# 600 slots per expert instead of 608, outputs turned in 64-row halves, and a plain product for the last tile of a threshold attention with hash-routed experts

## The chip, the core and the metric

The kernel runs on one core of a Trainium2 chip. The core has TensorE (PE: matrix products and transposes, with its weight loads shown as PEld), VectorE (DVE), ScalarE (ACT), GpSimd (POOL) and SyncE (SP); POOL and SP issue most of the DMAs. PE writes only PSUM; DVE and ACT bring results from PSUM to SBUF.

The metric is device time in microseconds. Three timed runs of the kernel before gave 958.95, 956.51 and 956.54: median 956.54 us. One more execution was recorded by the profiler, which lengthens it a little.

## What is computed

First attention with a threshold, for 8 batches, 8 heads, 576 positions and 64 dimensions: scores that lie more than `tau` under the largest of their row are left out. Its output, turned to 4608 rows of 512, goes through a mixture of 8 experts, in which the token's id alone picks the expert.

```python
scores = scale * np.matmul(q, k.transpose(0, 1, 3, 2))
thresh = np.max(scores, axis=-1, keepdims=True) - tau
scores = np.where(scores >= thresh, scores, -1000000000.0)
...
expert_idx = token_ids * np.int64(2654435761) % np.int64(E)
for e in range(E):
    mask = expert_idx == e
    xe = x[mask]
    h = np.maximum(xe @ w1[e], 0.0)      # w1[e]: 512 x 1024
    out[mask] = h @ w2[e]                # w2[e]: 1024 x 512
```

The inputs are made with a fixed seed. The experts get between 533 and 599 of the 4608 tokens.

## The kernel before

**Attention** takes about the first half. It goes over 32 pairs of heads in steps that are written out by hand; PE computes scores (L219), turns the weights in halves of 64 rows (`turn`, L260 to L267) and multiplies by `v` (L297), while DVE and ACT work on rows of 576. Between these steps the generator `route()` (L350) runs small DVE operations that give every token a slot: expert times `CAP` plus its rank in the expert. Tokens beyond `CAP` of an expert go to overflow tiles. `scatters()` (L483) writes each token's number into a table of slots in DRAM, and the table is read back in an order of blocks of 32 slots; copies on DVE make the index tiles `gidx` and `gidx_x` of it (L744 to L750).

**The experts** follow one another. An expert has `CAP` = 608 slots in 19 blocks of 32: five tiles of rows, of 128, 128, 128, 128 and 96. `gather` fetches the rows of `x` by an indirect DMA of POOL, DVE turns them in squares of 32 and SP moves the squares into `xT` (L908 to L923).

Each of the two layers of an expert is a two-by-two block product with seven block products in place of eight (`seven`, L825). The slots are cut in two halves of `CH` = 304 columns. `left` and `right` prepare the sums of blocks on DVE; `left` writes one of them, s1, over the block a21 of the weights. A block product fills a PSUM tile `bank2` (two banks; four such tiles) and DVE adds it up. After each of six steps `seven` calls a function that puts other work in between. Layer 1 makes `h_0` (1024 x 608), layer 2 makes `oT` (512 x 608). An expert has 2 x 56 matrix products of 304 columns, except expert 0, whose first layer is a plain product that begins beside attention (`early_h`, `late_h`).

**The output.** `put_out` (L876) turns a tile of `oT` with four transposes of 128x128 (L882), copies the result to `o_sb` (ACT at L890; for the last expert also DVE at L888), and `put_rows` (L893) scatters the rows to `out` by an indirect DMA of POOL. The tiles of expert e are put out during the first layer of expert e + 1: two after step 0, two after step 1, one after step 2. For the last expert, tiles 0 and 1 follow step 4 of its second layer and the others the end of it (L970, L977). All this stands under a manual schedule: instructions go to the engines in the order in which the code makes them.

**The overflow loop** (L989) comes last; it runs once for each overflow tile. With no overflow tile it is skipped, but POOL and the other engines still wait in its exit for all DMAs.

Of the kernel before, what the change touches and what calls it, by code (L numbers as in the profile page):

```python
# [9 lines left out]
FP32 = mybir.dt.float32  # L10
# [10 lines left out]
def kernel(  # L21
# [12 lines left out]
    nc = tc.nc  # L34
# [28 lines left out]
    NSLOT = -(-(E * CAP + NOV * P) // P) * P  # L63
    BIG = 1 << 20
# [63 lines left out]
    with tc.tile_pool(name="a_q", bufs=1) as a_q, \  # L128
# [221 lines left out]
        def route():  # L350
# [39 lines left out]
            for e in (0, E // 2):  # L390
# [6 lines left out]
                if e == 0:  # L397
# [54 lines left out]
            nc.vector.tensor_scalar(out=ovt[:], in0=ovt[:], scalar1=float(P),  # L452
                                    scalar2=float((E - 1) * CAP), op0=ALU.mult, op1=ALU.add)
            yield
# [28 lines left out]
        def scatters():  # L483

            for c in range(NTC):
                nc.gpsimd.indirect_dma_start(
                    out=slot_dram[c % 2][:, :],
                    out_offset=bass.IndirectOffsetOnAxis(ap=slot_i[:, c:c + 1], axis=0),
                    in_=tok[:, c:c + 1], in_offset=None, bounds_check=NSLOT - 1,
                    oob_is_err=False)  # L490
                yield
            for _ in range(4):
                yield
            for table, dst in zip(slot_dram, sidx):
                slots = table[0:CAP].rearrange("(c s) o -> c (s o)", c=32)
                for h in range(4):
                    nc.sync.dma_start(out=dst[32 * h:32 * h + 32, 0:(NB - h + 3) // 4],
                                      in_=slots[:, h::4])
            for table, dst in zip(slot_dram, (stok, stok_odd)):
                for h in range(HP):  # L500
                    nc.sync.dma_start(
                        out=dst[32 * h:32 * h + 32],
                        in_=table[0:E * CAP].rearrange("(e c s) o -> c e (s o)", e=E, c=32))
# [121 lines left out]
        with tc.manual_schedule():  # L625
# [133 lines left out]
    with tc.tile_pool(name="m_x", bufs=1) as m_x, \  # L759
# [5 lines left out]
        xq = m_x.tile([P, DIN // 32, 32 * KT], FP32, name="xq")  # L765
        oT = m_x.tile([P, CO, CAP], FP32, name="oT")
        mark = m_x.tile([P, 1], FP32, name="mark")
# [4 lines left out]
        p1, u2, u3, u4 = (m_s.tile([P, 2, CH], FP32, name=n) for n in ("p1", "u2", "u3", "u4"))  # L772

# [3 lines left out]
        def sub(out, in0, in1):  # L777
            return lambda: nc.vector.tensor_tensor(out=out, in0=in0, in1=in1, op=ALU.subtract)
# [3 lines left out]

        def left(a11, a12, a21, a22, s):

            s2, s3, s4 = s
            return [sub(s3, a11, a21), add(a21, a21, a22), sub(s2, a21, a11), sub(s4, a12, s2)]

# [13 lines left out]

        def h_blocks(c0, c1):
            return [h_0[:, FH * j + c0:FH * j + c1, CH * k:CH * k + CH]
                    for j in range(2) for k in range(2)]

        def triple(t, c0, c1):
            return [t[:, i, c0:c1] for i in range(3)]

# [3 lines left out]
        def sums_w2(e):  # L812
            return left(*w2_blocks(w_tiles[e, 2]), triple(w2_s, 0, FH))

        def sums_x(e):
            return right(*x_blocks(xT_bufs[e % 2]), triple(x_s, 0, C2))

        def sums_h(c0, c1):
            return right(*h_blocks(c0, c1), triple(h_s, c0, c1))

# [4 lines left out]
        def seven(a, a_s, b, b_s, m0, outs, relu, after):  # L825

            (a11, a12, s1, a22), (s2, s3, s4) = a, a_s
            (b11, t1, b21, b22), (t2, t3, t4) = b, b_s
            c11, c12, c21, c22 = outs
            n_k = a11.shape[1]  # L830

            def product(x, y):
                ps = bank2()
                for i in range(2):
                    c0 = m0 + P * i
                    for c in range(n_k):
                        nc.tensor.matmul(ps[:, i, 0:CH], lhsT=x[:, c, c0:c0 + P], rhs=y[:, c],  # L837
                                         start=c == 0, stop=c == n_k - 1)
                return ps[:, :, 0:CH]
# [7 lines left out]
            nc.scalar.copy(p1[:], product(a11, b11))  # L847
            out(c11, product(a12, b21), p1[:], 0)
            add(u2[:], product(s2, t2), p1[:])()
            after(1)  # L850
            add(u3[:], product(s3, t3), u2[:])()
            after(2)
            out(c21, product(a22, t4), u3[:], 3)
            k5 = product(s1, t1)
            add(u4[:], k5, u2[:])()
            out(c22, k5, u3[:], 4)
            out(c12, product(s4, b22), u4[:], 5)

# [9 lines left out]
        def layer2(e, side):  # L868

            w = w_tiles.pop((e, 2))  # L870
            outs = [oT[:, C2 * i:C2 * i + C2, CH * k:CH * k + CH]
                    for i in range(2) for k in range(2)]
            seven(w2_blocks(w), triple(w2_s, 0, FH), h_blocks(0, FH), triple(h_s, 0, FH), 0, outs,
                  False, side)

        def put_out(e, kts):  # L876

            tr = bank2()
            for i, kt in enumerate(kts):
                rows = TROWS[kt]  # L880
                for co in range(CO):
                    nc.tensor.transpose(tr[0:rows, i, P * co:P * co + P],  # L882
                                        oT[:, co, FIRST[kt]:FIRST[kt] + rows], ident[:])
            for i, kt in enumerate(kts):
                rows = TROWS[kt]
                o_sb = m_o.tile([P, DIN], FP32, name="o_sb")
                if e == E - 1 and kt % 2:
                    nc.vector.tensor_copy(o_sb[0:rows], tr[0:rows, i])  # L888
                else:
                    nc.scalar.copy(o_sb[0:rows], tr[0:rows, i])  # L890
                put_rows(o_sb[0:rows], gidx[0:rows, e, kt:kt + 1])
# [33 lines left out]
        with tc.tile_pool(name="ps_x", bufs=1, space=PSUM) as ps_x, tc.manual_schedule():  # L925
            run(sums_w2(0), 4)
            fill(18)
            late_h(lambda fo: (ps_sc.tile([P, 2, 512], FP32, name="sc") if fo in (2, 4) else
                               ps_x.tile([P, 2, 512], FP32, name="xT_ps")))
            fetch(1)  # L930
            run(sums_h(0, FH), 4)
        sc_stack.close()
        ps_m = [ctx.enter_context(tc.tile_pool(name="ps_m", bufs=4, space=PSUM))]

        with tc.manual_schedule():
            for e in range(E):
# [3 lines left out]
                if e > 0:  # L940
                    w2_work, h_work = sums_w2(e), sums_h(0, 2)

# [14 lines left out]
                    layer1(e, side1)  # L957
                    run(sums_h(2, FH), 4)
                if e + 2 < E:
# [3 lines left out]
                def side2(step):  # L963
# [25 lines left out]
        with tc.For_i(0, n_ov, 1) as it:  # L989
# [12 lines left out]
            for table, dst in zip(slot_dram, (idx, idx_odd)):  # L1002
                nc.gpsimd.dma_start(out=dst[:], in_=table[bass.ds(it * P + E * CAP, P), :])
            nc.vector.tensor_tensor(out=idx[:], in0=idx[:], in1=idx_odd[:], op=ALU.min)
# [48 lines left out]
```

## Time and profile before

| | |
|---|---|
| median of three runs | 956.54 us |
| the profiled execution | 963.93 us, its span 962.3 us |
| granted clock of TensorE | 0.997 |
| busy over the span: PE, PEld, DVE, ACT, POOL | 98%, 67%, 77%, 50%, 31% |
| attention, from the start to about | 475 us |
| end of expert 0's first layer, start of the block products | 503.9 us |
| the last block product ends about | 950.0 us |
| block products in all (L837) | 1680 records of PE |
| output transposes (L882) | 160 records, 273 ns each as shown |

An instruction of PE with 32-bit operands appears as two records when it is a product and as one when it is a transpose. Records of PE overlap in the pipeline, so that the length shown for one (419 ns for a product of 304 columns) is more than the distance to the next; the distance is what counts. In the profile's shapes, `64*128` is a product that uses 64 of the array's 128 rows, `128*64` one that uses 64 of its columns, and `128*128` one that uses all.

### The profile page before, as it was taken

The page shows a single profiled execution, that of the slowest core. Times are in us where ns is not written, and L with a number is a line of the kernel's source. Part 1 is how long each engine was busy: PE and PEld are TensorE (multiplying, and loading weights), DVE is VectorE, ACT ScalarE, POOL GpSimd, SP SyncE. Part 2 cuts the span into 40 slices and gives each one's busy share as a digit, 9 for nine tenths or more (in the row PEclk, how much of TensorE's full clock was granted, in tenths as well). Part 3 has the DMA queues.
Part 4 walks back from the last instruction along what each step waited for, and adds up shares of the span by engine and source line. Part 5 has one row for each costly group of instructions (what it writes and reads, how often), then busy time and mean ns, then how long its engine had stood idle before and what let it go on. Part 6 is the DMA issues. An engine that isn't in the chain of part 4 may idle for free.

```text
span 962.3 us, 20672 instructions
## 1 busy us (share of the span) xinstructions
PE 941.3 (98%) x7595; PEld 646.8 (67%) x7595; DVE 738.2 (77%) x1631; ACT 479.6 (50%) x777; POOL 302.4 (31%) x413
## 2 busy tenths in 40 slices
PE   7999999999999999999999999999999999999995
PEld 4666666666566666656667777777777777777774
DVE  8999999999999999999446666756657556675541
ACT  6988898888888888888220211202112031120310
POOL 4233233346666633564043300303013030100202
PEclk9999999999999999999999999999999999999998
DMA  7445445544546857631016444344433445211101
GB/s 181 97 121 146 116 111 141 135 111 110 125 99 177 212 154 199 157 93 32 26 45 208 161 106 159 95 141 161 129 127 103 140 152 158 108 53 25 50 1 50
DMA packets 113397, 113.41 MB, mean 118 GB/s; under 512 B 27476, under 2 KB 87896, under 8 KB 113296
## 3 DMA queue, kind: packets, MB, share of 16 engines
q1 hardware_dynamic: 105168, 92.95, 35.7%
q0 software_dynamic: 7696, 18.91, 6.4%
q8 instruction: 62, 1.02, 0.4%
q14 instruction: 39, 0.32, 0.1%
q10 hardware_dynamic: 432, 0.21, 0.1%
HBM read 81.99 MB, written 21.85 MB: 108 GB/s over the span
## 4 chain that ended last, share of the span: by engine, by line
PE 79%; issue 16%; DVE 1%; ACT 1%; POOL 1%; DMA 1%; SPq 0%; POOLq 0%; DVEq 0%; ACTq 0%
PE bank L837 29%; PE av L297 18%; PE sc L219 15%; PE tr L266 11%; PE sc L578 3%; PE av L266 2%; PE bank L882 1%; POOL out_dram L894 1%; ACT w L244 1%; DVE w L255 1%; PE xT_ps L595 0%; PE sc L595 0%; DVE ns L230 0%; ACT wT_b L287 0%; DMA out_dram<-o_sb,gidx 0%
## 5 line engine op out<-in xcount | busy, mean ns | idle before, releaser
L244 ACT ACTIVATE w<-ns,nmx 128x576 f32<-128x576 f32 x288 | 220.4, 777 | 27.0 <-DVE ns L230 26.8
L255 DVE SCALAR_TENSOR_TENSOR w<-ns,thr,w 128x576 f32<-128x576 f32 x288 | 225.4, 815 | 0.0
L230 DVE TENSOR_SCALAR_CACHE_REDUCE ns<-sc 128x576 f32<-128x576 f32 x288 | 205.6, 746 | 7.5 <-PE sc L219 6.7
L219 PE MATMUL sc<-k_sb,q 64*128 64x288 f32 (+1 forms) x1280 | 177.2, 421 | 1.2 <-DVE drop L641 0.5
L266 PEld LDWEIGHTS tr<-ident,w 64*128 64x128 f32 x2624 | 106.1, 139 | 95.5 <-ACT wT_b L287 32.2
L237 POOL TENSOR_SCALAR thr<-nmx,drop 128x2 f32<-128x2 f32 (+1 forms) x160 | 103.8, 649 | 189.3 <-DVE ns L230 176.7
L266 PE MATMUL tr<-ident,w 64*128 64x64 f32 x2624 | 139.6, 231 | 6.6 <-ACT wT_b L287 2.6
L894 POOL DMA_INDIRECT out_dram<-o_sb,gidx x40 | 47.9, 1198 | 302.0 <-ACT o_sb L890 294.7
L847 ACT COPY p<-bank 128x608 f32<-128x608 f32 x22 | 14.6, 665 | 205.1 <-PE bank L837 205.0
L219 PEld LDWEIGHTS sc<-k_sb,q 64*128 64x128 f32 (+1 forms) x1280 | 92.9, 177 | 21.8 <-DVE ns L230 8.1
L837 PE MATMUL bank<-h,w_sb 128*128 128x304 f32 x384 | 101.0, 419 | 0.9 <-DVE h L600 0.9
L297 PE MATMUL av<-wT_a,v 128*64 128x320 f32 (+1 forms) x704 | 100.4, 418 | 0.0
L844 ACT ACTIVATE h<-h 128x608 f32<-128x608 f32 x56 | 39.8, 710 | 114.6 <-DVE h L781 111.9
L287 ACT COPY wT_a<-tr 128x512 f32<-128x512 f32 (+1 forms) x128 | 81.7, 639 | 20.5 <-PE tr L266 20.2
L837 PEld LDWEIGHTS bank<-h,w_sb 128*128 128x128 f32 x384 | 72.9, 190 | 26.5 <-DVE h L600 1.4
L837 PE MATMUL bank<-xT,w_sb 128*128 128x304 f32 x336 | 90.5, 419 | 0.0
L287 ACT COPY wT_b<-tr 128x512 f32<-128x512 f32 (+1 forms) x128 | 81.3, 635 | 16.0 <-PE tr L266 8.9
L297 PE MATMUL av<-wT_b,v 128*64 128x256 f32 x640 | 83.2, 389 | 0.0
L837 PEld LDWEIGHTS bank<-xT,w_sb 128*128 128x128 f32 x336 | 63.8, 190 | 22.1
L837 PE MATMUL bank<-h_s,w_s 128*128 128x304 f32 x256 | 66.8, 419 | 0.0
L297 PEld LDWEIGHTS av<-wT_a,v 128*64 128x64 f32 x704 | 43.8, 136 | 28.5
L781 DVE TENSOR_TENSOR u<-bank,u 128x608 f32<-128x608 f32 x44 | 34.3, 780 | 35.1 <-PE bank L837 35.0
(139 smaller groups left out, 1141.0 us busy)
## 6 DMA issues: line engine op xcount, KB each, us to landing
w_sb<-in_moe_w_dram SPq DMA_DIRECT2D x16, 2048.0 KB
q<-in_q_dram SPq DMA_DIRECT2D x62, 288.0 KB
v<-in_v_dram SPq DMA_DIRECT2D x32, 256.0 KB
x_scratch<-xm SPq DMA_DIRECT2D x32, 256.0 KB
xT<-xq SPq DMA_DIRECT2D x84, 80.0 KB
k_sb<-in_k_dram SPq DMA_DIRECT2D x31, 144.0 KB
k_sb<-in_k_dram SPq DMA_DIRECT2D x32, 112.0 KB
x_scratch<-xg SPq DMA_DIRECT2D x9, 256.0 KB
```

The costliest lines, as they stand in the source:

```text
L219: nc.tensor.matmul(sc[out_rows, i, 0:S2], lhsT=q_sb[rows, h, q0:q1], rhs=k_sb[rows, h], start=True, stop=True)
L230: nc.vector.tensor_scalar(out=ns[:].rearrange("p (i s) -> p i s", i=2), in0=sc[:, :, 0:S2], scalar1=-1.0, scalar2=None, op0=ALU.mult, op1= ...
L237: nc.gpsimd.tensor_scalar(out=thr[:, 0:j + 1], in0=stats[n][0][:, 0:j + 1], scalar1=drop[:], scalar2=None, op0=ALU.add)
L244: nc.scalar.activation(w, nss[n, j][:], AF.Exp, bias=stats[n][0][:, j:j + 1], scale=-1.0)
L255: nc.vector.scalar_tensor_tensor(out=w, in0=nss.pop((n, j))[:], scalar=stats[n][1][:, j:j + 1], in1=w, op0=ALU.is_le, op1=ALU.mult, accum_ ...
L266: nc.tensor.transpose(dst[:, r, 64 * c:64 * c + 64], src[rows, c0:c0 + P], ident[rows, rows])
L287: nc.scalar.copy(dst, tr[:, :, 0:64 * n_c].rearrange("p r (c q) -> p r c q", c=n_c))
L297: nc.tensor.matmul(av[64 * j:64 * j + 64, g, c0:c1], lhsT=v_sb[:, c, 64 * j:64 * j + 64], rhs=wT[g][:, i, c0:c1], start=(c == 0), stop=stop)
L781: return lambda: nc.vector.tensor_tensor(out=out, in0=in0, in1=in1, op=ALU.add)
L837: nc.tensor.matmul(ps[:, i, 0:CH], lhsT=x[:, c, c0:c0 + P], rhs=y[:, c], start=c == 0, stop=c == n_k - 1)
L844: nc.scalar.activation(c, c, AF.Relu)
L894: inst = nc.gpsimd.indirect_dma_start(out=out[:, :], out_offset=bass.IndirectOffsetOnAxis(ap=idx, axis=0), in_=o_sb, in_offset=None, bound ...
```

## The change

- `CAP` becomes 600. The table keeps 19 blocks of 32 slots (`SL` = 608) for an expert, but the last block holds only 24: a slot's place skips one in 18 beyond rank 456. Three more DVE operations in `route()` compute that. The halves `CH` become 300 columns and the last tile has 88 rows.
- `put_out` turns each 128x128 piece as two pieces of 64 rows, which go to the two banks of the PSUM tile; the copies to `o_sb` put them together in runs of 64.
- For the last expert, layer 2 runs on 480 slots only (halves `CHL` = 240). The remaining 120 slots are a plain product with the slots as the stationary operand (`last_tile`), so that their output needs no transpose: 8 products of 384 columns, then 8 of 128. In the middle of the first eight, `put_out` turns tiles 1, 2 and 3. So that the plain product finds the weights unchanged, s1 of that expert goes to a spare buffer of `w1_sb`.
- `gidx` of the last expert's tile 4 gets the indexes of the last four blocks: four more small copies.

```diff
-    CAP = 32 * NB
+    SL = 32 * NB
+    CUT = 8
+    CAP = SL - CUT
+    FULL = NB * (32 - CUT)
...
+            nc.vector.tensor_scalar(out=rank_f[:], in0=rank[:], scalar1=float(-1 - FULL), scalar2=0.0,
+                                    op0=ALU.add, op1=ALU.max)
...
-            nc.vector.tensor_scalar(out=first[:], in0=eidf[:], scalar1=float(CAP), scalar2=None,
+            nc.vector.tensor_scalar(out=rank_i[:, 0], in0=rank_f[:], scalar1=57.0, scalar2=None,
                                     op0=ALU.mult)
+            nc.vector.tensor_scalar(out=rank_i[:, 0], in0=rank_i[:, 0], scalar1=10, scalar2=None,
+                                    op0=ALU.logical_shift_right)
...
+            nc.vector.scalar_tensor_tensor(out=first[:], in0=eidf[:], scalar=float(SL),
+                                           in1=rank_i[:, 0], op0=ALU.mult, op1=ALU.add)
...
+                nc.vector.tensor_copy(gidx[rows, E - 1, KT - 1:KT],
+                                      stok[rows, E - 1, NB - 4 + h:NB - 3 + h])
...
+        CHL = 32 * (NB - 4) // 2
...
+            s1 = None
+            if e == E - 1:
+                spare = w_pool.tile([P, CO, F], FP32, name="w1_sb")
+                s1 = w_tiles["s1"] = spare[:, :, 0:D2]
+            return left(*w2_blocks(w_tiles[e, 2]), triple(w2_s, 0, FH), s1)
...
+        def last_tile(middle):
+
+            w, o_sb, idx = w_tiles[E - 1, 2], o_end, gidx[:, E - 1, KT - 1:KT]
+            rows = CAP - 2 * CHL
+            for c0, c1 in ((0, DIN - P), (DIN - P, DIN)):
+                ps = bank2()
+                for fo in range(FO):
+                    nc.tensor.matmul(ps[0:rows, 0, 0:c1 - c0], lhsT=h_0[:, fo, 2 * CHL:CAP],
+                                     rhs=w[:, fo, c0:c1], start=fo == 0, stop=fo == FO - 1)
+                    if (c0, fo) == (0, FH - 1):
+                        middle()
+                nc.scalar.copy(o_sb[0:rows, c0:c1], ps[0:rows, 0, 0:c1 - c0])
+            put_rows(o_sb[0:rows], idx[0:rows])
...
-                    nc.tensor.transpose(tr[0:rows, i, P * co:P * co + P],
-                                        oT[:, co, FIRST[kt]:FIRST[kt] + rows], ident[:])
+                    for r in range(2):
+                        half, c0 = slice(64 * r, 64 * r + 64), D2 * i + 64 * co
+                        nc.tensor.transpose(tr[0:rows, r, c0:c0 + 64],
+                                            oT[half, co, FIRST[kt]:FIRST[kt] + rows],
+                                            ident[half, half])
...
+                dst = o_sb[0:rows].rearrange("p (c r q) -> p r c q", c=CO, r=2)
+                src = tr[0:rows, :, D2 * i:D2 * i + D2].rearrange("p r (c q) -> p r c q", c=CO)
...
-                        put_out(e, (0, 1))
+                        put_out(e, (0,))
...
-            put_out(E - 1, (2, 3))
-            put_out(E - 1, (4,))
+            def middle():
+                put_out(E - 1, (1, 2))
+                put_out(E - 1, (3,))
+
+            last_tile(middle)
```

More of the change, by code (lines that the diff above doesn't have):

```diff
@@ L62 @@
     NOV = 32
-    NSLOT = -(-(E * CAP + NOV * P) // P) * P
+    NSLOT = -(-(E * SL + NOV * P) // P) * P
     BIG = 1 << 20
@@ L446, in route @@
             nc.vector.tensor_copy(rank[:], rank_i[:, 1])
+            nc.vector.tensor_scalar(out=rank_f[:], in0=rank[:], scalar1=float(-1 - FULL), scalar2=0.0,
+                                    op0=ALU.add, op1=ALU.max)
             yield
             nc.vector.tensor_copy(ovt[:], rank_i[:, 2])
-            nc.vector.tensor_scalar(out=first[:], in0=eidf[:], scalar1=float(CAP), scalar2=None,
+            nc.vector.tensor_scalar(out=rank_i[:, 0], in0=rank_f[:], scalar1=57.0, scalar2=None,
                                     op0=ALU.mult)
+            nc.vector.tensor_scalar(out=rank_i[:, 0], in0=rank_i[:, 0], scalar1=10, scalar2=None,
+                                    op0=ALU.logical_shift_right)
             yield
             nc.vector.tensor_scalar(out=ovt[:], in0=ovt[:], scalar1=float(P),
-                                    scalar2=float((E - 1) * CAP), op0=ALU.mult, op1=ALU.add)
+                                    scalar2=float(E * SL - CAP), op0=ALU.mult, op1=ALU.add)
+            nc.vector.scalar_tensor_tensor(out=first[:], in0=eidf[:], scalar=float(SL),
+                                           in1=rank_i[:, 0], op0=ALU.mult, op1=ALU.add)
             yield
@@ L494, in scatters @@
             for table, dst in zip(slot_dram, sidx):
-                slots = table[0:CAP].rearrange("(c s) o -> c (s o)", c=32)
+                slots = table[0:SL].rearrange("(c s) o -> c (s o)", c=32)
                 for h in range(4):
@@ L502, in scatters @@
                         out=dst[32 * h:32 * h + 32],
-                        in_=table[0:E * CAP].rearrange("(e c s) o -> c e (s o)", e=E, c=32))
+                        in_=table[0:E * SL].rearrange("(e c s) o -> c e (s o)", e=E, c=32))
             for _ in range(4):
@@ L766 @@
         oT = m_x.tile([P, CO, CAP], FP32, name="oT")
+        o_end = m_x.tile([P, DIN], FP32, name="o_end")
         mark = m_x.tile([P, 1], FP32, name="mark")
@@ L771 @@
         h_s = m_s.tile([P, 3, FH, CH], FP32, name="h_s")
-        p1, u2, u3, u4 = (m_s.tile([P, 2, CH], FP32, name=n) for n in ("p1", "u2", "u3", "u4"))
+        halves = [m_s.tile([P, 2, CH], FP32, name=n) for n in ("p1", "u2", "u3", "u4")]
+        CHL = 32 * (NB - 4) // 2
         def bank2():
@@ L781, in add, with left @@
             return lambda: nc.vector.tensor_tensor(out=out, in0=in0, in1=in1, op=ALU.add)
-        def left(a11, a12, a21, a22, s):
+        def left(a11, a12, a21, a22, s, s1=None):
+            s1 = a21 if s1 is None else s1
             s2, s3, s4 = s
-            return [sub(s3, a11, a21), add(a21, a21, a22), sub(s2, a21, a11), sub(s4, a12, s2)]
+            return [sub(s3, a11, a21), add(s1, a21, a22), sub(s2, s1, a11), sub(s4, a12, s2)]
         def right(b11, b12, b21, b22, t):
@@ L800, in x_blocks, with h_blocks, triple, half2 @@
             return [x[:, C2 * j:C2 * j + C2, CH * k:CH * k + CH] for j in range(2) for k in range(2)]
-        def h_blocks(c0, c1):
-            return [h_0[:, FH * j + c0:FH * j + c1, CH * k:CH * k + CH]
+        def h_blocks(c0, c1, half):
+            return [h_0[:, FH * j + c0:FH * j + c1, half * k:half * k + half]
                     for j in range(2) for k in range(2)]
-        def triple(t, c0, c1):
-            return [t[:, i, c0:c1] for i in range(3)]
+        def triple(t, c0, c1, width=None):
+            return [t[:, i, c0:c1, 0:width] for i in range(3)]
+        def half2(e):
+            return CH if e < E - 1 else CHL
         def sums_w1(e):
@@ L812, in sums_w2, with sums_h @@
         def sums_w2(e):
[L813 removed]
+            s1 = None
[3 more added lines that the diff above has]
+            return left(*w2_blocks(w_tiles[e, 2]), triple(w2_s, 0, FH), s1)
         def sums_x(e):
             return right(*x_blocks(xT_bufs[e % 2]), triple(x_s, 0, C2))
[L818 to L819 removed]
+        def sums_h(e, c0, c1):
+            return right(*h_blocks(c0, c1, half2(e)), triple(h_s, c0, c1, half2(e)))
         def run(work, n=1):
@@ L829, in seven @@
             c11, c12, c21, c22 = outs
-            n_k = a11.shape[1]
+            n_k, width = a11.shape[1], b11.shape[2]
+            p1, u2, u3, u4 = (t[:, :, 0:width] for t in halves)
             def product(x, y):
@@ L836, in product @@
                     for c in range(n_k):
-                        nc.tensor.matmul(ps[:, i, 0:CH], lhsT=x[:, c, c0:c0 + P], rhs=y[:, c],
+                        nc.tensor.matmul(ps[:, i, 0:width], lhsT=x[:, c, c0:c0 + P], rhs=y[:, c],
                                          start=c == 0, stop=c == n_k - 1)
-                return ps[:, :, 0:CH]
+                return ps[:, :, 0:width]
             def out(c, ps, u, step):
@@ L845, in out @@
                 after(step)
-            nc.scalar.copy(p1[:], product(a11, b11))
-            out(c11, product(a12, b21), p1[:], 0)
-            add(u2[:], product(s2, t2), p1[:])()
+            nc.scalar.copy(p1, product(a11, b11))
+            out(c11, product(a12, b21), p1, 0)
+            add(u2, product(s2, t2), p1)()
             after(1)
-            add(u3[:], product(s3, t3), u2[:])()
+            add(u3, product(s3, t3), u2)()
             after(2)
-            out(c21, product(a22, t4), u3[:], 3)
+            out(c21, product(a22, t4), u3, 3)
             k5 = product(s1, t1)
-            add(u4[:], k5, u2[:])()
-            out(c22, k5, u3[:], 4)
-            out(c12, product(s4, b22), u4[:], 5)
+            add(u4, k5, u2)()
+            out(c22, k5, u3, 4)
+            out(c12, product(s4, b22), u4, 5)
         def layer1(e, side):
@@ L868, in layer2 @@
         def layer2(e, side):
-            w = w_tiles.pop((e, 2))
-            outs = [oT[:, C2 * i:C2 * i + C2, CH * k:CH * k + CH]
+            w, half = w_tiles[e, 2], half2(e)
+            outs = [oT[:, C2 * i:C2 * i + C2, half * k:half * k + half]
                     for i in range(2) for k in range(2)]
-            seven(w2_blocks(w), triple(w2_s, 0, FH), h_blocks(0, FH), triple(h_s, 0, FH), 0, outs,
-                  False, side)
+            a = w2_blocks(w)
+            if e == E - 1:
+                a[2] = w_tiles["s1"]
+            seven(a, triple(w2_s, 0, FH), h_blocks(0, FH, half),
+                  triple(h_s, 0, FH, half), 0, outs, False, side)
+        def last_tile(middle):
[10 more added lines that the diff above has]
+            put_rows(o_sb[0:rows], idx[0:rows])
         def put_out(e, kts):
@@ L879, in put_out @@
             for i, kt in enumerate(kts):
-                rows = TROWS[kt]
+                rows = TROWS[kt] if e < E - 1 or kt < KT - 2 else 2 * CHL - FIRST[kt]
                 for co in range(CO):
-                    nc.tensor.transpose(tr[0:rows, i, P * co:P * co + P],
-                                        oT[:, co, FIRST[kt]:FIRST[kt] + rows], ident[:])
+                    for r in range(2):
[3 more added lines that the diff above has]
+                                            ident[half, half])
             for i, kt in enumerate(kts):
-                rows = TROWS[kt]
+                rows = TROWS[kt] if e < E - 1 or kt < KT - 2 else 2 * CHL - FIRST[kt]
                 o_sb = m_o.tile([P, DIN], FP32, name="o_sb")
+                dst = o_sb[0:rows].rearrange("p (c r q) -> p r c q", c=CO, r=2)
+                src = tr[0:rows, :, D2 * i:D2 * i + D2].rearrange("p r (c q) -> p r c q", c=CO)
                 if e == E - 1 and kt % 2:
-                    nc.vector.tensor_copy(o_sb[0:rows], tr[0:rows, i])
+                    nc.vector.tensor_copy(dst, src)
                 else:
-                    nc.scalar.copy(o_sb[0:rows], tr[0:rows, i])
+                    nc.scalar.copy(dst, src)
                 put_rows(o_sb[0:rows], gidx[0:rows, e, kt:kt + 1])
@@ L930 @@
             fetch(1)
-            run(sums_h(0, FH), 4)
+            run(sums_h(0, 0, FH), 4)
         sc_stack.close()
@@ L940 @@
                 if e > 0:
-                    w2_work, h_work = sums_w2(e), sums_h(0, 2)
+                    w2_work, h_work = sums_w2(e), sums_h(e, 0, 2)
                     def side1(g, step):
@@ L957 @@
                     layer1(e, side1)
-                    run(sums_h(2, FH), 4)
+                    run(sums_h(e, 2, FH), 4)
                 if e + 2 < E:
@@ L1002 @@
             for table, dst in zip(slot_dram, (idx, idx_odd)):
-                nc.gpsimd.dma_start(out=dst[:], in_=table[bass.ds(it * P + E * CAP, P), :])
+                nc.gpsimd.dma_start(out=dst[:], in_=table[bass.ds(it * P + E * SL, P), :])
             nc.vector.tensor_tensor(out=idx[:], in0=idx[:], in1=idx_odd[:], op=ALU.min)
```

## The prediction, made before the changed kernel was run

> **What bounds the kernel.** I read three views, in this order: the busy time by stretches, the chain that ended last, and the timeline around the calls that the change edits. All durations are from the one profiled execution (963.93 us, span 962.3); the median of the three runs shown, 956.54 us, is 7.4 us lower. I take differences from the profiled one and subtract them from the median.
>
> The first fence is the busy time by stretches: time of the stretch, then PE, PEld, DVE, ACT, POOL, each with its count of records. The first line is attention, the second all eight experts.
>
> ```profile
> 120.00:180.00 60.00, 59.90 (x746) 37.75 (x742) 59.98 (x171) 53.16 (x87) 19.61 (x35) 1.00 0.53 131
> 503.90:950.00 446.10, 446.10 (x1828) 334.12 (x1828) 271.96 (x333) 74.55 (x115) 79.89 (x70) 1.00 0.36 113
> ```
>
> In attention PE and DVE are both full. In the experts PE is full at the whole clock (1.00) and DVE, ACT and POOL have at least 39% to spare: there, time is what PE is given to do. The next fence is the chain across one expert (start, length, engine, tile, line, records).
>
> ```profile
> 543.16 53.22 PE bank L837 x208
> 596.38 0.87 PE bank L882 x8
> 597.25 2.05 PE bank L837 x8
> 599.30 0.87 PE bank L882 x8
> 600.17 2.05 PE bank L837 x8
> 602.22 0.44 PE bank L882 x4
> 602.66 7.42 PE bank L837 x29
> ```
>
> There is no gap. An expert is 112 products, each shown as two records of 304 columns: 224 records. 53.22 / 208 is 255.9 ns a record. A full 128x128 transpose is one record: 0.87 / 8 is 109 ns. So 224 x 0.2559 + 20 x 0.109 = 59.5 us, the distance from 537.75 to 597.25, where the same record stands one expert apart. Between the two kinds lie 176 columns and 147 ns, so a record costs 0.834 ns a column plus 2.3 ns: 252.5 ns at 300 columns, 202.5 at 240, 322.6 at 384, 109 at 128.
>
> **Part 1, 600 columns in place of 608.** Experts 1 to 7 run layer 1 and experts 0 to 6 layer 2 at 300: 14 x 112 = 1568 records, 3.34 ns less each: **-5.2 us**, all on the path. Expert 0's first layer, begun beside attention and finished before 503.9, has 128 records: 0.43 us, of which a little lies beside waits for ACT and DVE: **-0.35**. DVE and ACT operations shrink by 8 columns off the path: nothing.
>
> **Part 2, outputs turned in halves, experts 0 to 6.** 20 transposes become 40 of 64 rows, alternating between the halves of the array. The trace has this form in attention, and next to products that use the whole array (timeline: start, length, engine, line, operation):
>
> ```profile
> 249.45 0.53 PE L266 MATMUL tr<-ident,w 64*128 64x64 f32 x10
> 249.81 1.19 PE L219 MATMUL sc<-k_sb,q 64*128 64x288 f32 x8
> ...
> 463.26 1.29 PE L578 MATMUL sc<-xT,w_sb 128*128 128x304 f32 x4
> 464.48 0.46 PE L266 MATMUL tr<-ident,w 64*128 64x64 f32 x8
> 464.88 0.78 PE L578 MATMUL sc<-xT,w_sb 128*128 128x304 f32 x2
> ```
>
> From start to start, ten halves before another half-array operation take 0.36 us: 36 ns each. Runs of 8 take 0.25 to 0.30, the one of 24 (L554) 0.75: 31 to 37 ns. Two halves then cost about 67 to 73 ns against 109. But four full-array records take 1.22 us from 463.26 to 464.48, where 4 x 0.2559 is 1.02: 0.20 us going in. Eight halves take 0.40 coming out, 0.10 over the unswitched run. The first fence on the chain shows no such price around full transposes. So a call pays 0.30 us for the two changes. A call of 8 full transposes (0.87) becomes 16 halves at some 33 ns (0.53) + 0.30 = 0.83; the call of 4 (0.44) becomes 0.28 + 0.30 = 0.58. Per expert 2 x (-0.04) + 0.14 = +0.06; seven experts: **+0.4 us**. Ends: -0.4 at 31 ns, +2 if each entry is like the one near 465.68 (0.29).
>
> Here two rules of the Trainium skill pull apart. TensorEngine Tiling (Array Packing), Theoretical Speedup, promises up to 2x where the contraction is 64 or less: 140 transposes x 54.5 ns would give -7.6 us. The same page, Key Properties, says that changing the tiling mode, not just the tile, drains TensorE. The rows above put 0.30 us on that drain, and it is paid 21 times for short runs, so I take +0.4.
>
> The copies out of PSUM keep 512 elements, now in runs of 64. ACT's copy of that form in attention (L287) is 0.58 us, as now (582 ns). ACT is 83% idle here; no cost.
>
> **Part 3, expert 7 and the end.** Take t = 0 at the first product of its layer 2 (920.45 on PE's row); the span ends at 41.85.
> Now 112 x 202.5 ns = 22.68; tile 0 in 8 halves with both changes 0.58: 23.26. Four plain products of 384 columns, 8 x 322.6 = 2.58: 25.84. They cover the last sum on DVE (0.2 us after PE, then under 0.79), which now stops PE for 0.88. Change of mode 0.20 and 16 halves 0.55: tiles 1 and 2 stand in PSUM at 26.6. DVE copies tile 1 (0.2 to see it, then 0.69): 27.5. ACT copies tile 2 after it, because the built program has it wait for DVE: 28.1. DMA issue starts 0.28 after a copy and repeats every 1.28, as here:
>
> ```profile
> 952.77 0.69 DVE L888 COPY o_sb<-bank 128x512 f32<-128x512 f32 x1 [1.80 <-ACT o_sb L890]
> 953.02 0.98 POOL L894 DMA_INDIRECT out_dram<-o_sb,gidx  x1 [3.80 <-ACT o_sb L890]
> 954.30 0.98 POOL L894 DMA_INDIRECT out_dram<-o_sb,gidx  x1 [0.30 <-issue]
> 955.58 0.93 POOL L894 DMA_INDIRECT out_dram<-o_sb,gidx  x1 [0.30 <-DMA out_dram<-o_sb,gidx]
> ```
>
> So tiles 1, 2, 3 are issued at 27.8, 29.1, 30.4. Beside that PE ends the plain product: 8 halves 0.28, mode 0.10, 8 x 322.6, 16 x 109 = 1.75: at 31.4; ACT's copy of 128 columns (its 256-column copies, L313, take 0.36) is done by 31.9.
> The diff does not tell where the fifth scatter goes. In the order of the built program it stands **behind the overflow loop**, in a block of its own after the loop's exit, whose waits cover every earlier DMA and engine. Queued behind those waits is nothing else. POOL's queue today (name, count, length, first and last start):
>
> ```profile
> L989 POOLq EVENT_SEMAPHORE  x16: 17/43/1605, 955.0 to 959.1; - x16
> L1049 POOLq DRAIN  x3: 46/103/2118, 959.4 to 962.0; - x3
> ```
>
> From the last issue (955.58) to the end block (959.37) are 3.79 us: landing, then twelve waits. After the change: 30.4 + 3.79 = 34.2; an extra branch 0.3 (estimate, PE's dearest branch row is 0.31); the issue 1.0; then the end block's 2.9 us (drain 2.12 and barriers): 38.4. Gain 41.85 - 38.4 = **-3.4 us**. Ends: -4.5 if the drain is mostly a code fetch that runs beside the issue, -0.5 if the new block costs its own fetch and the drain waits for the landing (2.7 us from issue).
>
> **Part 4, routing.** Three more operations of 36 columns on DVE near 173 to 187 us, where it is full. Such rows take 0.17 us and repeat every 0.09, or 0.23 where one needs the other: 0 to 0.6, taken as **+0.35**; some falls into DVE's gaps (about 8 us over 60 to 440). The four extra gidx copies (at most 0.2 each, like L747's 0.77 for four) stand at 476.4 on DVE ahead of the copy of expert 0's third block (479.25), which PE needs by about 481.2: covered; 0.7 us at most if not. The spare w1 buffer is expert 6's, last read some 30 us earlier: no wait.
>
> **Sum:** -5.2 - 0.35 + 0.4 - 3.4 + 0.35 = **-8.2 us**: 955.7 for a profiled execution, **948.3 us** as median.
>
> **Rivals.**
> A, the forecast: 948.3, own range 946.8 to 949.8. Chance 0.68.
> B, the halves pay no change of mode in the experts: 21 x 0.30 off part 2 and 0.9 off the end: 941.1 if no call pays, 944.7 if half of them do. For it: halves at 36 ns are real. Against: each of the four crossings with full-array products shows the price. Chance 0.12.
> C, the end gives nothing: the moved scatter's own landing and a code fetch stand bare behind the exit, so part 3 is -0.5: 951.2. For it: an instruction fetch lies near 960.4 in the queues, inside the drain. Against: the drain and barriers are long enough to hold a landing. Chance 0.16.
> D, slower: the change of mode in `put_out`. With 23 switched calls (21, and two in the end) it cancels the other gains at 0.30 + 8.2 / 23 = 0.66 us a call; at 1.0 us a call the time is 964.4. For it: the skill's drain, and these calls follow accumulating products, unlike most in the trace. Against: the dearest crossing here is under half of that. Chance 0.04.
> That the change does not do what it says, an expert with over 600 tokens, would add an overflow pass of 4.2 MB of weights, 20 us at the page's best 212 GB/s; counting the reference's fixed token ids modulo 8 gives 599 for the fullest, so it gets no chance.
>
> **Numbers.** 0.3% is 2.9 us: about what a measurement can tell. A, B and C are all below 953.7. Faster 0.95, same 0.02 and slower 0.03 (D split by its price). Range 943.0 to 952.0: A, most of C, and of B what lies above two thirds of its full gain.
>
> **What would show it.** 1568 records near 252.5 ns and an expert period of 58.8 us; L923 calls with 0.2 before and 0.1 after; tile scatters of the end 1.28 apart, then one lone scatter at least 3.5 us behind them, after the loop's waits; an end at 38.4 us from layer 2's start. A period under 58.3 says B; an end beyond 40.5 says C; a period above 59.5 says D.

## The result and the profile after

| | before | after |
|---|---|---|
| median of five runs each, same chip | 956.99 us | 950.61 us |
| range | 956.51 to 958.95 | 949.84 to 952.65 |
| the profiled execution, its span | 963.93, 962.3 | 951.87, 950.2 |

The ratio is 0.9932, with a 95% interval of 0.992 to 0.9944: 6.4 us less. The forecast was 948.3 us in a range of 943.0 to 952.0, faster with a chance of 0.95.

The two profiled spans differ by 12.1 us, nearly twice what the timed runs do. It isn't the profiler that lengthens an execution: the profiled one of the changed kernel, 951.87 us, lies inside the range of its timed runs. Laid out by stage, from the start of one named group of records to the next:

| stage | before | after | difference | forecast |
|---|---|---|---|---|
| start to expert 0's first layer | 460.96 | 455.95 | -5.01 | +0.35 |
| expert 0's first layer, to the first block product | 42.91 | 42.46 | -0.45 | -0.35 |
| block products, to the last layer 2 | 416.59 | 411.70 | -4.89 | -5.2 + 0.4 |
| last layer 2 to the end | 41.87 | 40.06 | -1.81 | -3.4 |

The first row isn't the change's: the last section shows that attention took some 5 us more in some profiles than in others, with and without the change. What the change does there can be read from two of attention's 32 steps, counted from one run of its output transposes (`av<-ident,oT` on PE) to the next. The eleventh and the twelfth, from about 172 us on, take 13.99 us each in both profiles of the kernel before, and 14.32 and 14.15 in all twelve profiles with the new routing, each to 0.01: 0.49 us more. So the sum by stages is +0.49 - 0.45 - 4.89 - 1.81 = -6.7 us, and the timed runs gave -6.4.

This is the busy time by stretches, the columns as before: attention, the experts up to 10 us ahead of the end, and the last layer 2 with what follows it.

```profile
120.00:180.00 60.00, 59.89 (x740) 37.20 (x734) 59.93 (x172) 51.97 (x85) 19.59 (x36) 1.00 0.55 131
503.90:940.00 436.10, 436.10 (x1992) 327.79 (x1991) 264.60 (x332) 73.45 (x115) 77.11 (x68) 1.00 0.36 112
910.11:950.17 40.06, 31.41 (x177) 26.88 (x175) 9.20 (x14) 3.57 (x7) 4.94 (x5) 0.95 0.09 30
```

PE is still full in both big stretches, at the full clock; more records (1992) stand in the second because a transpose is now two. In the third PE is done after 31.41 of 40.06 us: in the remaining 8.65 us only a last copy on ACT (0.27 us), POOL and the DMAs have work.

The next fence is PE's timeline across one expert (start, length, line, tile, shape, records), from the first layer of expert 1, in which the outputs of expert 0 are turned, to the same place one expert on.

```profile
526.80 4.20 PE L859 MATMUL bank<-xT,w_sb 128*128 128x300 f32 x16
530.93 0.71 PE L923 MATMUL bank<-ident,oT 64*128 64x64 f32 x16
531.58 2.29 PE L859 MATMUL bank<-x_s,w_s 128*128 128x300 f32 x8
533.79 0.71 PE L923 MATMUL bank<-ident,oT 64*128 64x64 f32 x16
534.43 2.29 PE L859 MATMUL bank<-x_s,w_s 128*128 128x300 f32 x8
536.65 0.43 PE L923 MATMUL bank<-ident,oT 64*88 64x64 f32 x8
537.01 2.29 PE L859 MATMUL bank<-x_s,w_sb 128*128 128x300 f32 x8
539.13 2.19 PE L859 MATMUL bank<-xT,w_sb 128*128 128x300 f32 x8
541.15 2.18 PE L859 MATMUL bank<-xT,w_s 128*128 128x300 f32 x8
543.17 4.20 PE L859 MATMUL bank<-xT,w_sb 128*128 128x300 f32 x16
547.21 4.21 PE L859 MATMUL bank<-x_s,w_s 128*128 128x300 f32 x16
...
589.73 0.72 PE L923 MATMUL bank<-ident,oT 64*128 64x64 f32 x16
```

Read the distances of the starts, not the lengths. From 543.17 to 547.21 are 4.04 us for 16 records of 300 columns: 252.5 ns each, the figure that the line through the old rows gave. From 530.93 to 589.73 are 58.80 us: the period that was forecast. The change between the two forms (the change of tiling mode, in the prediction's words) costs time on either side of the halves. Eight records at 252.5 ns are 2.02 us. The run ahead of the first call only goes in and takes 0.09 more (4.13 for sixteen); the run behind the last call only comes out and takes 0.10 more (2.12). The two runs between the calls come out of one call and go into the next, and take 0.19 and 0.20 more (531.58 to 533.79, 534.43 to 536.65). So it is 0.10 us at each edge.

The end, as the timeline of all engines (what an engine waited for stands in brackets):

```profile
910.11 6.64 PE L859 MATMUL bank<-h,w_sb 128*128 128x240 f32 x32
...
933.39 2.74 PE L908 MATMUL bank<-w_sb,h 128*120 128x384 f32 x8
936.06 0.94 PE L923 MATMUL bank<-ident,oT 64*128 64x64 f32 x24
936.93 4.59 PE L908 MATMUL bank<-w_sb,h 128*120 128x384 f32 x24
937.79 0.98 POOL L938 DMA_INDIRECT out_dram<-o_sb,gidx  x1 [5.77 <-DVE o_sb L932]
939.08 0.98 POOL L938 DMA_INDIRECT out_dram<-o_sb,gidx  x1 [0.30 <-issue]
940.36 0.95 POOL L938 DMA_INDIRECT out_dram<-o_sb,gidx  x1 [0.30 <-issue]
941.55 0.27 ACT L912 COPY o_end<-bank 120x128 f32<-120x128 f32 x1 [1.27 <-PE bank L908]
944.94 1.02 POOL L938 DMA_INDIRECT out_dram<-o_end,gidx  x1 [3.63 <-issue]
```

With 910.11 as zero the scatters of tiles 1, 2 and 3 start at 27.7, 29.0 and 30.25, the last copy is over at 31.7, and the lone scatter starts at 34.83, after the exit of the overflow loop. What comes then is in POOL's queue (name, count, least / median / greatest length in ns, first and last start):

```profile
L1038 POOLq EVENT_SEMAPHORE  x16: 17/43/1545, 939.6 to 943.9; - x16
```

and, by the line of the drain:

```profile
L1098 POOLq DRAIN  x3: 46/109/4632, 944.7 to 949.9; - x3
```

The waits of the exit are over at 34.0, as forecast (34.2). DRAIN is the instruction in POOL's queue on which the end of the kernel stands; the longest of the three was 2118 ns before and is **4632 ns** now. It begins at 944.7, ahead of the lone scatter, so the scatter's issue lies inside it; but from the end of that issue to the end of the drain are still 3.36 us. Most of the 1.6 us that the end is longer than forecast are there.

### The profile page after: what moved, and what is told of

It reads as the page before. It is cut to its first block, busy times and chain, and to the rows that moved or that the text cites. A ratio compares the mean times of both kernels' runs of the same rounds, so it can differ in the third digit from the quotient of the medians.

```text
span 950.2 us, 21041 instructions
## 1 busy us (share of the span) xinstructions
PE 935.2 (98%) x7779; PEld 645.2 (68%) x7779; DVE 733.9 (77%) x1638; ACT 478.6 (50%) x778; POOL 306.2 (32%) x413
## 5 line engine op out<-in xcount | busy, mean ns | idle before, releaser
L869 ACT COPY p<-bank 128x600 f32<-128x600 f32 (+1 forms) x22 | 14.4, 654 | 201.4 <-PE bank L859 200.6
L859 PE MATMUL bank<-h,w_sb 128*128 128x300 f32 (+1 forms) x384 | 97.3, 410 | 0.9 <-DVE h L609 0.9
L866 ACT ACTIVATE h<-h 128x600 f32<-128x600 f32 x56 | 39.4, 703 | 114.6 <-DVE h L794 114.1
L859 PE MATMUL bank<-xT,w_sb 128*128 128x300 f32 x336 | 89.4, 416 | 0.0
L859 PE MATMUL bank<-h_s,w_s 128*128 128x300 f32 (+1 forms) x256 | 64.3, 410 | 0.0
L859 PE MATMUL bank<-x_s,w_s 128*128 128x300 f32 x224 | 61.5, 423 | 0.0
```

The costliest lines, as they stand in the source:

```text
L859: nc.tensor.matmul(ps[:, i, 0:width], lhsT=x[:, c, c0:c0 + P], rhs=y[:, c], start=c == 0, stop=c == n_k - 1)
L869: nc.scalar.copy(p1, product(a11, b11))
```

## The experiments

Two questions were open. Why is the drain of the end longer: because the lone scatter lies in front of it, because the new block behind the loop costs something of its own, or because a fixed time follows POOL's last instruction? And is the small gain of the halves really eaten by changes of mode, as the forecast has it, against rival B? Each diff is against the changed kernel unless it is said otherwise, and `...` stands where lines are left out. "Mid" is the time from the first block product to the last layer 2, "end" the time from there to the end of the span; both are read from one profile of each kernel.

The runs used three chips. e_front, e_block, e_full and e_before ran on the first, where the kernel before took 963.93 us (median of 19 runs, 960.87 to 967.32); e_width, e_cut0, e_onecall and e_best on the second, where it took 956.86 (25 runs, 956.37 to 959.68); e_nolone, e_pad2, e_pad4 and e_fullone, with one run each, on the third, where its single run took 956.53. The changed kernel itself isn't among these runs, so a ratio here is always to the kernel before.

### The lone scatter ahead of the loop's exit (e_front)

```diff
             last_tile(middle)
+            n_ov = nc.values_load(ov_i[0:1, NOV:NOV + 1], min_val=0, max_val=NOV)
...
-        n_ov = nc.values_load(ov_i[0:1, NOV:NOV + 1], min_val=0, max_val=NOV)
```

> The changed kernel with the overflow count's register loads written inside the manual schedule, behind the last tile; in the built program this puts the last scatter ahead of the overflow loop, nothing else moves. Theory 1 (POOL's drain at the very end waits for the scatter that stands just ahead of it): the scatter starts at 32.0 us after the start of the last layer 2, the drain is back at 2.1 us (4.63 in the changed kernel), the span ends 38.7 us after that start (40.1), and the time falls by about 1.4 us to 949.2. Theory 2 (the longer drain comes from the place of the code, not from the scatter): the drain stays over 4 us and the time stays at 950.6.

957.2 us (955.62 to 959.39), ratio 0.9935 (0.9913 to 0.9957). Mid 411.70, end 39.68. POOL's timeline of this kernel, and then its drain in POOL's queue:

```profile
945.93 0.95 POOL L938 DMA_INDIRECT out_dram<-o_sb,gidx  x1 [0.30 <-issue]
947.68 1.02 POOL L938 DMA_INDIRECT out_dram<-o_end,gidx  x1 [0.80 <-issue]
```

```profile
L1098 POOLq DRAIN  x3: 46/103/2200, 952.3 to 955.1; - x3
```

The scatter moved from 34.83 to 32.01, and the drain is at 2200 ns, near the 2118 of the kernel before. But the end fell by 0.38 us only, a miss: the wait went from the drain into the exit, which now stands until this scatter has landed, 3.57 us after its start (947.68 to 951.25). A scatter at the end is waited for on either side of the exit.

### The block behind the exit, with something else than a scatter in it (e_block)

Here the scatter stays ahead of the exit, as in e_front, and POOL copies one element behind the loop.

```diff
+        nc.gpsimd.tensor_copy(mark[0:1, :], h_0[0:1, 0, 0:1])
```

> As e_front, but with a copy of one element on POOL behind the loop, so that a block of its own still stands there, without a scatter in it. Theory 1 (the drain waits for the scatter): drain 2.1 us, end about 0.5 us behind e_front's. Theory 2 (the block's code costs it, as a fetch): drain over 4 us, as in the changed kernel.

957.34 us in one run; end 40.0. POOL's timeline and its drain:

```profile
952.39 0.18 POOL L1068 COPY mark<-h 1x1 f32<-1x1 f32 x1 [3.72 <-issue]
```

```profile
L1099 POOLq DRAIN  x3: 46/109/2418, 952.4 to 955.4; - x3
```

The drain is 2418 ns: a block with an instruction in it adds 0.2 to 0.3 us to it, not 2.5. An instruction fetch (a packet of 8 KB in a DMA queue of its own) isn't what makes the long drain long either: in the changed kernel this packet is over at 35.25, counted as above, 3.97 us ahead of the drain's end at 39.22.

### The changed kernel without the lone scatter (e_nolone)

The rows of the last tile (120, not 88 as the expectation has it) are computed but not written.

```diff
                 nc.scalar.copy(o_sb[0:rows, c0:c1], ps[0:rows, 0, 0:c1 - c0])
-            put_rows(o_sb[0:rows], idx[0:rows])
```

> The changed kernel without the lone scatter: the 88 rows of the last tile are computed but not written. If the scatter is what lengthens the drain, the drain is 2.1 to 2.4 us again and the end is 37.6 us from the last layer 2's start (exit at 34.0, branch 0.6, then 2.96 as before). If the block behind the exit costs a fetch of its own, it stays above 39.

947.9 us in one run; end 36.97. Its drain:

```profile
L1097 POOLq DRAIN  x3: 46/103/2118, 943.1 to 945.8; - x3
```

2118 ns, to the nanosecond that of the kernel before. The lone scatter, with the block in which it stands, costs 40.06 - 36.97 = **3.1 us** of the end. The forecast had given it 1.3 (0.3 for the branch, 1.0 for the issue), and without these its sum is 38.4 - 1.3 = 37.1: the rest of the end was forecast right.

### Work of POOL behind the lone scatter (e_pad2, e_pad4)

```diff
+        nc.gpsimd.memset(h_0[:, 0:2], 0.0)
```

> A memset of POOL over 1200 columns (estimate 1.1 us, from 0.333 us at 288 and 0.204 at 128 columns) behind the lone scatter, in the same block; it writes h_0, which nothing reads any more. Landing theory (the last drain waits until the scatter has landed): the end stays at 40.1 us from the last layer 2's start. Fixed-time theory (the drain takes 3.4 us after POOL's last instruction): the end moves with the memset, to 41.2.

and the same with `h_0[:, 0:4]`:

> The same with 2400 columns (estimate 2.2 us). Landing theory: the memset is over some 1.1 us ahead of the drain's end in the changed kernel, so the end stays at 40.1; if the landing is only part of the 3.4 us and a fixed tail follows it, up to 0.7 more. Fixed-time theory: 42.3.

POOL's timeline, then the drain in its queue, with 1200 columns:

```profile
944.11 1.02 POOL L938 DMA_INDIRECT out_dram<-o_end,gidx  x1 [3.65 <-issue]
945.11 1.13 POOL L1068 MEMSET h<- 128x1200 f32 x1
```

```profile
L1099 POOLq DRAIN  x3: 46/109/4622, 943.9 to 949.1; - x3
```

and the two with 2400:

```profile
942.72 1.02 POOL L938 DMA_INDIRECT out_dram<-o_end,gidx  x1 [3.63 <-issue]
943.72 2.13 POOL L1068 MEMSET h<- 128x2400 f32 x1
```

```profile
L1099 POOLq DRAIN  x3: 46/109/5578, 942.5 to 948.6; - x3
```

With 1.13 us of work more, the drain is as long as without it (4622 against 4632 ns) and the end is 40.11: the theory of a fixed time of 3.4 us after POOL's last instruction falls. With 2.13 us it grows by 0.95, and the end is 41.04, over the 40.8 that the landing with a fixed tail allowed. So two things run side by side, and the later one counts: what the scatter needs, and some 2.2 us after POOL's last instruction (945.85, the end of the memset, to 948.07, the end of the drain; 2.27 with the shorter memset, where both meet; 2.23 in e_block, behind its copy).

What the scatter needs could still be a time from its issue or from its landing (the end of its last packet), since in these kernels the last packet always ends 2.91 to 2.94 us after the issue begins. The next experiment happens to separate them.

### Nothing narrower: 608 slots with the rest of the change (e_cut0)

```diff
-    CUT = 8
+    CUT = 0
```

> The changed kernel with 608 slots: halves and plain last tile (128 rows) stay, only the width is undone. Theory 1: period 59.56 us (+0.06 over before, the change of the array's mode less what the halves save), 416.9 us to the last layer 2, end 40.1 us after its start; about 1.0 us less than before, within the noise of the runs. Theory 2 (halves and end carry the gain): 3 us or more less than before.

955.41 us (954.9 to 956.82, 21 runs), ratio 0.9985 (0.9978 to 0.9991). Mid 417.02: 0.43 more than before, from the halves. End 39.36, earlier than expected by 0.7: its drain is shorter.

```profile
L1098 POOLq DRAIN  x3: 46/109/4009, 948.2 to 952.8; - x3
```

The lone scatter has 128 rows here in place of 120, and by the packets' records its last packet ends 2.36 us after the issue begins, not 2.91. The drain ends 1.42 us after that packet; in the changed kernel and with the shorter memset it is 1.47. From the start of the issue it is 3.79 against 4.38. So the drain follows the **landing**, as far as one kernel with another landing can show it. This also says what the narrowing itself is worth: everything else of the change gives 1.45 us (956.86 - 955.41), where the whole gave 6.4.

### The narrowing alone (e_width)

Full 128x128 transposes, layer 2 of expert 7 as before, `put_out` calls as before, no extra `gidx` copies.

```diff
-            return CH if e < E - 1 else CHL
+            return CH
...
-            def middle():
-                put_out(E - 1, (1, 2))
-                put_out(E - 1, (3,))
-
-            last_tile(middle)
+            put_out(E - 1, (2, 3))
+            put_out(E - 1, (4,))
```

> Only the 600 slots of the change: full 128x128 transposes and the end as before. Theory 1 (a product's record costs 0.834 ns a column, so the 8 columns are paid in full): period of an expert 58.73 us (59.50 before), block products from first to the last layer 2 in 411.4 us (416.6), end 41.5 us after its start (41.9), routing +0.47, in all 5.6 us less than before. Theory 2 (the time lies elsewhere, for instance in the attention stretch that the changed kernel's first profile ran faster): less than half of that.

952.08 us (951.46 to 952.81), ratio 0.9952 (0.9938 to 0.9966): 4.8 us of the 6.4. Mid 411.36 as expected, 5.23 less than before. End 41.91, where 41.5 was expected. The last scatter starts 0.37 us sooner (34.76 for 35.13), but the drain starts at 38.87 for 38.91: from the start of the issue to the last packet it is 2.69 us in place of 2.35, so the landing took the gain back.

### Full transposes in the changed kernel, and the kernel before once more (e_full, e_before)

```diff
-                    for r in range(2):
-                        half, c0 = slice(64 * r, 64 * r + 64), D2 * i + 64 * co
-                        nc.tensor.transpose(tr[0:rows, r, c0:c0 + 64],
-                                            oT[half, co, FIRST[kt]:FIRST[kt] + rows],
-                                            ident[half, half])
+                    nc.tensor.transpose(tr[0:rows, i, P * co:P * co + P],
+                                        oT[:, co, FIRST[kt]:FIRST[kt] + rows], ident[:])
...
-                dst = o_sb[0:rows].rearrange("p (c r q) -> p r c q", c=CO, r=2)
-                src = tr[0:rows, :, D2 * i:D2 * i + D2].rearrange("p r (c q) -> p r c q", c=CO)
+                dst, src = o_sb[0:rows], tr[0:rows, i]
```

> The changed kernel with full 128x128 transposes and plain copies in put_out, as before; 600 slots and the plain last tile stay. Theory 1 (each of the 21 calls pays 0.20 us to enter and 0.10 to leave the half-array mode, which eats what the halves save): expert period 58.73 us against 58.80, in all -0.4 us in the experts and +0.1 in the end, 950.3. Theory 2 (the halves carry a good part of the gain): period 59.0 or more, time 952 or more.

958.03 us (955.14 to 961.64), ratio 0.9941 (0.9925 to 0.9957); mid 411.36, end 40.17. Full transposes are **0.34 us cheaper** than the halves over seven experts, and 0.11 dearer in the end. The times can't tell the two kernels apart: the ratio of the changed one, on its own chip, is 0.992 to 0.9944.

The kernel before, profiled again on that chip:

> The kernel before, profiled again, unchanged. Theory 1 (attention in the first profile was stretched by chance, as the timed runs lie 7 us below it): the experts' block products start near 498 to 500 us, not at 503.9, and the span is 955 to 958; their period is again 59.50 us. Theory 2 (the change makes attention shorter by 5 us): start at 503.9 again and a span near 962.

962.56 us in one run; mid 416.59 and end 41.88, the same as in its first profile to 0.01 us. These two stages can be compared across chips; the stage of attention can't. The first theory's numbers miss: the block products start at 502.5 us and the span is 961.0, near the first profile's. But the second theory doesn't follow, since on this chip three kernels with the change reach expert 0's first layer at 461.5 to 462.4 us and the kernel before at 459.6: the change makes attention no shorter.

### One call per expert (e_onecall, e_fullone)

All 40 halves of an expert are turned in one run, then copied and scattered; three more buffers for `o_sb`.

```diff
-         tc.tile_pool(name="m_o", bufs=3) as m_o, \
+         tc.tile_pool(name="m_o", bufs=6) as m_o, \
...
+        def put_all(e, groups):
+            trs = [turn_out(e, kts) for kts in groups]
+            for tr, kts in zip(trs, groups):
+                copy_out(e, kts, tr)
...
                             if step == 0:
-                                put_out(e - 1, (0, 1))
-                            elif step == 1:
-                                put_out(e - 1, (2, 3))
-                            elif step == 2:
-                                put_out(e - 1, (4,))
+                                put_all(e - 1, ((0, 1), (2, 3), (4,)))
```

> The changed kernel with the five output tiles of an expert turned in one run after step 0 of layer 1, in place of three calls after steps 0, 1 and 2, with six o_sb buffers in place of three; so one entry into the half-array mode per expert in place of three. Theory 1 (0.20 to enter and 0.10 to leave, per call, is the price): the 40 halves take about 1.4 us and the entry 0.2: period 58.15 us against 58.80, 4.4 us less in seven experts. Theory 2 (no price per change of mode): 58.80 as before. Theory 3 (three PSUM tiles taken at once stall the block products): over 58.80.

946.06 us (945.44 to 947.52), ratio 0.9893 (0.9878 to 0.9908). Mid 406.99: 4.71 us less than the changed kernel. PE's timeline:

```profile
525.16 4.20 PE L859 MATMUL bank<-xT,w_sb 128*128 128x300 f32 x16
529.29 1.44 PE L931 MATMUL bank<-ident,oT 64*128 64x64 f32 x40
530.66 4.31 PE L859 MATMUL bank<-x_s,w_s 128*128 128x300 f32 x16
534.80 2.18 PE L859 MATMUL bank<-x_s,w_sb 128*128 128x300 f32 x8
```

The 40 halves take 1.37 us, 34 ns each; the products lose 0.09 ahead of them and 0.10 behind (4.13 and 4.14 for sixteen records, in place of 4.04). Two pairs of mode changes fewer in each of seven experts are 4.71 / 14 = **0.34 us a pair**. Of that 0.20 are at the two edges. The other 0.14 lie in the runs of halves themselves, which last 0.65 + 0.64 + 0.36 = 1.65 us in three calls and 1.37 in one. The rival explanation is that a call costs something whatever its transposes are; so the same with full transposes:

> One call per expert in place of three, but with full 128x128 transposes, which change no mode. Mode theory (what one call saved with halves is two changes of mode per expert): nothing is saved here, 411.4 us from the start of the block products to the last layer 2, as with full transposes in three calls. Rival (the calls themselves cost, whatever their transposes): 407 to 409.

953.63 us in one run; mid 411.32, against 411.36 with full transposes in three calls. Only 0.04 us is saved: it is the mode, not the call.

```profile
528.93 4.20 PE L859 MATMUL bank<-xT,w_sb 128*128 128x300 f32 x16
532.97 2.35 PE L929 MATMUL bank<-ident,oT 128*128 128x128 f32 x20
535.16 4.21 PE L859 MATMUL bank<-x_s,w_s 128*128 128x300 f32 x16
```

The sixteen records on either side take what sixteen records take (4.04 ahead of the transposes). 20 transposes are 2.19 us.

### The best of them (e_best)

One call per expert, and the lone scatter ahead of the exit.

> e_onecall with the last scatter ahead of the overflow loop. If one run of transposes pays (theory 1): period 58.15, end 39.7 us after the start of the last layer 2, about 4.8 us under the changed kernel, 11 us under the kernel before. If PSUM stalls: no better than the changed kernel.

**945.39 us** (944.53 to 946.76), ratio 0.9881 (0.9866 to 0.9896); mid 406.98, end 39.67. It has the lowest median and the lowest ratio of all that ran; what it has over one call per expert alone is within what these runs tell apart.

## Why the prediction was right, point by point

- **Part 1, the narrower products: right.** 252.5 ns a record, and with full transposes 5.23 us off the block products (forecast 5.2). Expert 0's first layer gave 0.45 for 0.35. The line through two kinds of record (0.834 ns a column and 2.3 ns) held where no record had stood before.
- **Part 2, the halves: right in size, wrong in where it is paid.** They cost 0.34 us over seven experts (forecast +0.4), and a pair of changes costs 0.34 (forecast 0.30). But the 0.20 read from the old trace as the price of going in was the price of both edges: those four products (463.26 to 464.48) stand between two runs of halves. It is 0.10 going in, 0.10 coming out, and the rest lies in the run of halves. The rule of the Trainium skill (TensorEngine Tiling (Array Packing), Key Properties) that a change of tiling mode drains TensorE fits: in the experts, products lose time next to such a change and none next to full transposes. The up to twofold speed of the same page (Theoretical Speedup) shows in part, 40 halves in 1.37 us where 20 full transposes take 2.19, and can be had only if one pair of changes carries many of them. Rival B falls. Of rival D the mechanism is real and its price stayed at half of what it needed (0.66 a call).
- **Part 3, the end: right in its order, wrong in one term.** The scatters stood at 27.7, 29.0 and 30.25 (forecast 27.8, 29.1, 30.4), the lone one behind the loop's exit, the exit over at 34.0 (34.2). The term that failed is "then the end block's 2.9 us (drain 2.12 and barriers)", taken unchanged from the kernel before. From the end of the lone scatter's issue to the end of the span are 4.21 us (35.85 to 40.06), 1.3 more, and from the exit to the scatter's start 0.83 in place of 0.3. In the kernel before, all scatters had landed ahead of the drain; in the changed one, the drain lasts until 1.47 us after the landing. The prediction had this in its outer end of the range for part 3 (-0.5), together with a code fetch, which the runs don't show to cost anything; measured is -1.8. Some 0.55 of the 1.3 come from a landing that is slow for its size: 2.91 us after the start of the issue, where the 128 rows of e_cut0 took 2.36.
- **Part 4, the routing: right in size** (+0.49 for +0.35), read from two steps of attention. The four extra `gidx` copies and the spare weights left no mark: PE has no gap in the experts.
- **Sum.** -6.7 by stages for -8.2; of the 1.5 us between, 1.6 are the end. Taken from this comparison's median before, 956.99, the 6.7 give 950.3; measured are 950.61. That is inside the range, but outside rival A's own 946.8 to 949.8 and close to C's 951.2. C had the right place and about half of its size came true; of its two reasons, the bare landing holds and the fetch doesn't.

## What to carry to other kernels

Short transposes in another tiling mode pay for the switch at both ends: gather them into one run before judging them. Here the same 40 halves lose 0.05 us an expert in three calls and win 0.6 in one. And when the last transfer is moved behind the last wait, its landing is not saved but moved: ask which instruction has to see it land, and take the time from the issue to there, not the issue alone.

## What the runs showed of the hardware

- POOL's last drain ended 1.42 to 1.47 us after the last packet of an indirect scatter that was still under way (six profiles), or some 2.2 us after POOL's last instruction (e_pad4, e_block), whichever came later. What the drain does inside isn't in the trace.
- A scatter of 120 rows took longer to move than one of 128: its packets lasted 1.31 us (issued at 944.94, 946.54 to 947.86) against 0.80 (`CUT` at 0: 950.02 to 950.82), with 80 packets each and fewer bytes (0.234 against 0.246 MB). So did the 88 rows of e_width against the 96 of the kernel before (e_before): 1.10 us in 80 packets against 0.86 in 64. No run tells why.
- Attention differs by about 5 us, and here it goes with the chip. On the first chip all four profiles needed 459.6 to 462.4 us to expert 0's first layer, with the kernel before as the fastest of them; on the two other chips all eight needed 453.7 to 458.1. The timed runs of the kernel before differ in the same way (963.93 against 956.86 and 956.53). The slow profiles lose it in the steps beside POOL's indirect DMAs (nearly all 14.0 to 15.9 us a step, one 17.6, in place of 13.89). On which chip the first profile of the kernel before was taken isn't on record; its 460.96 us is like those of the first chip. Why one chip is slower there is open, so only stages and ratios on one chip were compared.
